# Keys and queries of both chunks transposed together, and one schedule for attention and both blocks

## The chip, the cores and the metric

The kernel runs on one core of a Trainium2 chip. The metric is the device time of one execution, in microseconds. Matrix products and transposes run on TensorE (PE in the profile; its weight loads are PEld), elementwise work on VectorE (DVE) and ScalarE (ACT), a few small copies on GpSimd (POOL), and SyncE (SP) issues all transfers.

## The reference

A linear attention with a complex decay per token and channel, followed by two blocks on the 3072 tokens x 384 channels that it gives: a gated one (SiLU) and one with the maximum of three products. All arithmetic is float32.

```python
def _attn_ref(q, k, v, a_re, a_im):        # 4 batches, 8 heads, 768 tokens, 48 channels
    mag = np.sqrt(a_re * a_re + a_im * a_im)
    scale = np.minimum(mag, 0.999) / (mag + 1e-06)
    a_re_n, a_im_n = (a_re * scale, a_im * scale)
    ...
    for t in range(S):
        new_re = ar * S_re - ai * S_im
        new_im = ar * S_im + ai * S_re
        kv = np.einsum('bhd,bhe->bhde', k[:, :, t], v[:, :, t])
        S_re, S_im = (new_re + kv, new_im)
        y[:, :, t] = np.einsum('bhd,bhde->bhe', q[:, :, t], S_re)
def _moe_ref(x, w_gate, w_val, w_out):     # 384 -> 1536 -> 384
    g = x @ w_gate
    return (g / (1 + np.exp(-g)) * (x @ w_val)) @ w_out
def _moe2_ref(x, w1, w2, w3, w_out):       # 384 -> 768 -> 384
    return np.maximum(np.maximum(x @ w1, x @ w2), x @ w3) @ w_out
```

## The kernel before

**The attention** is done in 12 units (`u`), three for each batch. A unit is 256 tokens of all 8 heads, two chunks of 128 tokens. Partition 64c + 8h + s of a unit's tiles holds chunk `c`, head `h` and block `s` of 16 consecutive tokens; the free axis holds the 16 tokens, real and imaginary part, and 48 channels. `decay` normalizes the decays and multiplies them up inside blocks; `prefix` transposes the blocks' totals on PE (`tq<-bt`), scans them on DVE, and `unfold` transposes the result back (`tq<-I`); `queries_keys` multiplies the scanned decays into queries (`Q`) and keys (in place, in `A`) and sends the keys to `kn` by 16 transfers. `attend` turns queries and keys so that the 96 rows of real and imaginary channels lie on partitions (`tp`, copied by ACT to `QT` and `KT`), and then for each chunk multiplies keys by queries (`sc`), masks on DVE (`P`), updates the state (`xs`) and forms the output (`ys`), which ACT copies to `xr`; heads 6 and 7 reach it through `y67` and six transfers.

In `turn` (line 920) one chunk is turned at a time: PE transposes 64 partitions x 96 columns, eight of them into one bank of PSUM, and ACT copies the bank with the tokens reordered. A unit takes four such groups for its queries and four for its keys, 768 transposes in the program. PSUM has 8 banks: `tq`, `tp`, `sc` and `ys` have one each, `acc` two, `g` and `v` one each.

**The first block** (`Moe1`) takes a unit's `xr` as soon as it is there: `make_x` splits it in a rounded part `xh` (ACT) and the rest `xl` (DVE), and `moe1_group` goes through six slices `f` of 256 hidden columns: `g` and `v` (18 matmuls each), SiLU on ACT, the product `sg` and the split `hh`, `hl`, and 18 matmuls into `acc`. Every product takes three matmuls, of rounded parts and rests. The weights come as 64-bit floats; DVE, ACT and in part PE convert and split them (`split_w`) in the first stage. **The second block** (`Moe2`) does the same for 512 tokens at a time: three products into `p`, maximum into `hs`, and 4 x 3 matmuls per hidden slice into four accumulators, which leave by `ot`.

**What sets the order.** `Plan` records every operation as a task (hence all of them have one line in the profile) and writes each engine's stream by a list schedule: of the tasks that are ready by estimated costs, the one with the longest remaining path goes first. On PE, an attention task that is ready goes first, and of the two blocks' tasks that are ready the one with the lowest turn number. Tiles with one tag share a ring of `bufs` buffers, in the order in which the program asks for them. Before, there are two such plans: the first ends with the attention of the last unit and the first block of units 0 to 9; then the attention's memory is given back, and the second plan holds the first block of units 10 and 11 and the whole second block.

Of the kernel before, what the change touches and what calls it, by code (L numbers as in the profile page):

```python
# [75 lines left out]
class Plan:  # L76
# [7 lines left out]
    PSUM_TAGS = ("g", "v", "acc", "tq", "tp", "sc", "ys", "p", "po0", "po1")  # L84
# [3 lines left out]
    def __init__(self, nc, direct=False):  # L88
        self.nc, self.direct = nc, direct
        self.tasks, self.tags, self.open = [], {}, None  # L90
        self.free = {e: 0.0 for e in self.LAT}
        self.free["sync"] = 0.65
        self.table = None
        self.moved = self.busy = 0.0
        self.tick, self.warm = -1, False
        self.raw = []

# [111 lines left out]
    def schedule(self):  # L209
# [19 lines left out]
        while True:  # L229
# [23 lines left out]
            t = self.tasks[i]  # L253
            if e in ("vector", "scalar", "gpsimd"):
# [167 lines left out]
class Moe1:  # L422
# [20 lines left out]
    def load(self, s):  # L443
        f0 = s * SL
        if self.packed is not None:
            DM = self.src["o"].shape[1]
            for n, a, c in (("g", self.KD, SL), ("v", self.KD, SL), ("o", 2, DM)):
# [67 lines left out]
class Moe2:  # L515
# [7 lines left out]
    def __init__(self, P, place, xplace, oplace, mp, pf, ws, wo, packed=None):  # L523
        self.packed = packed
        self.P, self.place, self.xplace, self.oplace, self.mp, self.pf = P, place, xplace, oplace, mp, pf
# [4 lines left out]

    def load(self, s):
        if self.packed is not None:
            for n, a, c in (("1", self.KD, SL), ("2", self.KD, SL), ("3", self.KD, SL), ("o", 2, self.DM)):
                self.wt[n, s] = load_packed(self.P, *self.place(n, s), a, c, self.packed[n][s])
            return
        for n in "123":
            x, m = cols(self.src[n], SL * s, SL)
            self.wt[n, s] = load_w(self.P, *self.place(n, s), self.KD, SL, (
                (0, 128, x.rearrange("(j p) f -> p j f", p=128)),), m)
        x, m = words(self.src["o"])  # L540
        self.wt["o", s] = load_w(self.P, *self.place("o", s), 2, self.DM, (
            (0, 128, x[SL * s:SL * s + SL].rearrange("(j p) e -> p j e", p=128)),), m)
# [16 lines left out]
    def hid(self, g, f, turn):  # L559
        P, mp, U = self.P, self.mp, self.U  # L560
        xh, xl = self.x[g]
        s, o = divmod(128 * f, SL)
        hs = P.tile(mp, [128, U], F32, "hs", 2)
        for n in "123":
            p = P.tile(self.pf, [128, U], F32, "p", 2)
# [10 lines left out]
        hh = P.tile(mp, [128, U], F32R, "h2h", 2)  # L576
        hl = P.tile(mp, [128, U], F32R, "h2l", 2)
        P.copy(hh, hs, U)
        P.split_lo("vector", hl, hs, hh, U)
        self.h[g, f] = hh, hl  # L580

    def out(self, g, f, turn, dst):
        P = self.P
        hh, hl = self.h.pop((g, f))
        w = self.wt["o", f // 2]
        for t in range(self.U // 128):
            if f == 0:
                pool, tag = self.oplace(t)
                self.acc[g, t] = P.tile(pool, [128, self.DM], F32, tag)
            ps, ts = self.acc[g, t], slice(128 * t, 128 * t + 128)  # L590
            P.task("tensor", turn)
            P.mm3(ps, (hh[:, ts], hl[:, ts]), (w[:, f % 2, 0], w[:, f % 2, 1]), f == 0, f == self.KF - 1, self.DM)
            P.close()
            if f == self.KF - 1:
                ot = P.tile(self.mp, [128, self.DM], F32, "ot", 2)
# [4 lines left out]
def general_path(tc, q, k, v, a_re, a_im, w_gate, w_val, w_out, w1, w2, w3, w2_out, out):  # L600
# [94 lines left out]
    with ExitStack() as s2:  # L695
# [4 lines left out]
        m2 = Moe2(P, lambda n, s: (wp, f"y{n}{s}"), lambda n, g: (mp, f"x2{n}"), lambda t: (po, f"po{t}"),  # L700
                  mp, pf, (w1, w2, w3), w2_out)
# [15 lines left out]
def attn_moe_kernel(ctx, tc, q, k, v, a_re, a_im, w_gate, w_val, w_out, w1, w2, w3, w2_out,  # L717
# [52 lines left out]
    def load_a(u):  # L770
        A = A_t[u] = T([128, L, 2, D], "A", 3)
# [52 lines left out]
    def prefix(u):  # L824
# [3 lines left out]
        pt = T([NP, 2, 128], "tq", 1, patt)  # L828
# [4 lines left out]
        t1, t2 = T([NP, 2, G, 8], "tt1"), T([NP, 2, G, 8], "tt2")  # L833
# [32 lines left out]
    def unfold(u):  # L866

        pt = T([128, 2, D], "tq", 1, patt)
# [291 lines left out]
```

## Time and profile before

| | |
|---|---|
| time, three runs | 1070.1, 1072.82, 1078.19 us |
| the profiled execution, its own time | 1078.24 us |
| its span, first to last instruction | 1076.5 us |
| mean granted TensorE clock | 0.974 |
| PE busy | 1008.0 us, 7607 matmuls |
| DVE busy | 712.7 us |
| ACT busy | 487.5 us |

The shares are means over stages that differ: in the first 92 us decays and weights are prepared, to 655 us attention and first block run side by side, to 765 us the first block of the last two units, and then the second block alone. A stage is read by its window, and a wait by the instruction that ended it.

### The profile page before, as it was taken

What the parts mean: (1) busy time and instruction counts of PE and PEld (TensorE: products, weight loads), DVE (VectorE), ACT (ScalarE), POOL (GpSimd) and SP (SyncE); (2) the same over time, 40 slices, a digit from 0 to 9 for tenths busy, and PEclk for the clock granted to TensorE, in tenths of its full rate; (3) what the DMA queues carried; (4) which work ended last, traced back from release to release, by engine and by line L of the source; (5) the groups of instructions that cost most, each with busy time, mean ns of one, the idle gap of its engine ahead of it and who ended that gap; (6) DMA issues with size and microseconds to landing.
All of it is one profiled execution on the core that took longest, in us unless ns stands there. A gap on an engine that the chain in (4) does not pass through costs nothing.

```text
span 1076.5 us, 18718 instructions
## 1 busy us (share of the span) xinstructions
PE 1008.0 (94%) x7607; PEld 925.2 (86%) x7607; DVE 712.7 (66%) x1551; ACT 487.5 (45%) x762; POOL 5.0 (0%) x31
## 2 busy tenths in 40 slices
PE   0596999979999999999999999999999999999996
PEld 0476998879999999999999999999988888888885
DVE  6989999897988787888778984488322232222221
ACT  4454755656656565666566555234212121221211
POOL 0000000000000000000000000000000000000000
PEclk9968999989999999999999999999999999999998
DMA  9630211303130303040303032344101010100000
GB/s 380 250 91 19 56 53 45 97 27 97 31 103 25 102 8 115 3 121 13 112 3 82 13 82 42 108 177 162 45 1 59 1 59 1 59 15 16 30 1 32
DMA packets 52799, 73.54 MB, mean 68 GB/s; under 512 B 29281, under 2 KB 45793, under 8 KB 52705
## 3 DMA queue, kind: packets, MB, share of 16 engines
q1 hardware_dynamic: 52704, 72.27, 21.2%
q8 instruction: 61, 1.00, 0.4%
q14 instruction: 34, 0.27, 0.1%
HBM read 52.20 MB, written 9.44 MB: 57 GB/s over the span
## 4 chain that ended last, share of the span: by engine, by line
PE 87%; DVE 7%; ACT 2%; DMA 2%; issue 1%; SPq 1%; ACTq 0%; DVEq 0%
PE p L176 21%; PE v L176 16%; PE g L176 16%; PE acc L176 15%; PE ys L176 6%; PE tp L176 5%; PE sc L176 4%; PE po L176 3%; DVE A L176 2%; DVE s L176 2%; DVE t L176 1%; DMA A<-in_a_u_dram 1%; ACT s L176 1%; SPq L176 1%; DVE xo L176 0%
## 5 line engine op out<-in xcount | busy, mean ns | idle before, releaser
L176 PE MATMUL g<-xh,wg 128*128 128x256 f32 x864 | 178.9, 291 | 8.4 <-ACT xh L176 7.4
L176 PE MATMUL acc<-hh,wo 128*128 128x256 f32 x864 | 176.2, 290 | 1.2 <-DVE wo L176 0.7
L176 PE MATMUL v<-xh,wv 128*128 128x256 f32 x864 | 175.1, 289 | 2.2 <-DVE sg L176 2.2
L176 DVE TENSOR_TENSOR hs<-hs,p 128x512 f32<-128x512 f32 x72 | 49.5, 688 | 190.2 <-PE p L176 190.2
L176 PEld LDWEIGHTS g<-xh,wg 128*128 128x128 f32 x864 | 144.2, 195 | 11.8 <-ACT xh L176 7.9
L176 PEld LDWEIGHTS v<-xh,wv 128*128 128x128 f32 x864 | 142.4, 194 | 5.2 <-DVE sg L176 2.4
L176 PEld LDWEIGHTS acc<-hh,wo 128*128 128x128 f32 x864 | 142.0, 193 | 4.9 <-DVE wo L176 1.1
L176 PE MATMUL g<-xl,wg 128*128 128x256 f32 x432 | 124.2, 287 | 4.5 <-DVE xl L176 4.5
L176 PE MATMUL acc<-hl,wo 128*128 128x256 f32 x432 | 123.0, 285 | 0.1
L176 PE MATMUL v<-xl,wv 128*128 128x256 f32 x432 | 123.1, 285 | 0.0
L176 PE MATMUL p<-wv,y 128*128 128x512 f32 x324 | 112.4, 395 | 0.0
L176 ACT CAST hh<-sg 128x512 fp32r<-128x512 f32 x72 | 44.6, 620 | 109.4 <-PE acc L176 101.3
L176 DVE TENSOR_TENSOR sg<-sg,v 128x512 f32<-128x512 f32 x72 | 49.4, 686 | 60.4 <-PE v L176 46.9
L176 PEld LDWEIGHTS g<-xl,wg 128*128 128x128 f32 x432 | 84.2, 195 | 5.4 <-DVE xl L176 5.3
L176 ACT CAST h2h<-hs 128x512 fp32r<-128x512 f32 x36 | 22.4, 621 | 140.2 <-DVE hs L176 140.2
L176 PEld LDWEIGHTS acc<-hl,wo 128*128 128x128 f32 x432 | 83.5, 193 | 0.4 <-DVE hl L176 0.3
L176 PEld LDWEIGHTS v<-xl,wv 128*128 128x128 f32 x432 | 83.8, 194 | 0.0
L176 PEld LDWEIGHTS p<-wv,y 128*128 128x128 f32 x324 | 60.8, 188 | 13.7
L176 ACT ACT_TABLE_LOAD x53 | 68.0, 1283 | 5.7 <-DVE hl L176 2.6
L176 PE MATMUL p<-wg,y 128*128 128x512 f32 x216 | 69.7, 394 | 0.0
L176 ACT COPY KT<-tp 96x512 f32<-96x512 f32 x48 | 50.3, 1048 | 38.4 <-PE tp L176 21.3
L176 ACT ACTIVATE sg<-g 128x512 f32<-128x512 f32 x72 | 43.1, 598 | 44.7 <-PE g L176 38.2
(195 smaller groups left out, 1928.3 us busy)
## 6 DMA issues: line engine op xcount, KB each, us to landing
A<-in_a_u_dram SPq DMA_DIRECT2D x12, 768.0 KB
qk<-in_qk_u_dram SPq DMA_DIRECT2D x12, 768.0 KB
kn<-A SPq DMA_DIRECT2D x192, 48.0 KB
vt<-in_v_u_dram SPq DMA_DIRECT2D x24, 204.0 KB
wg<-in_moe_w_gate_s_dram SPq DMA_DIRECT2D x6, 768.0 KB
wv<-in_moe_w_val_s_dram SPq DMA_DIRECT2D x6, 768.0 KB
wo<-in_moe_w_out_s_dram SPq DMA_DIRECT2D x6, 768.0 KB
x2d<-xo SPq DMA_DIRECT2D x12, 384.0 KB
```

What stands on the lines that cost most here:

```text
L176: getattr(getattr(self.nc, eng), name)(**k)
```

## The change

- `turn` takes both chunks together: 128 partitions x 96 columns a transpose, four of them in one bank; eight are one task and fill two banks (`tp` has two, and `tq` is gone: the transposes of `prefix` and `unfold` take `tp` too). 384 transposes take the place of 768. ACT makes four copies of 512 columns for the queries of a unit and four for the keys, from a bank read across its four transposes to runs of four words.
- The whole program is one list schedule. The second block's weights and tiles take buffers of the attention (`A0`, `A1`, `qk`, `QT`, `KT`, `P`, `t3`, ...) and of the first block's weights, and `p` and two accumulators take banks of the attention.
- `A` has two buffers for units in turn (before three), `xr` two (before one), `ot` four (before two); the scan's `tt1`, `tt2` come from the ring `s3` of the decays. The weights' conversion rotates four buffers, two of them in the place of the last `wo`, which is therefore loaded later.
- The order in which a unit's parts are asked for is `U0 Q0 A0 D1 P1` throughout, and the planner counts 0.27 us for a change of kind on PE.

```diff
-    PSUM_TAGS = ("g", "v", "acc", "tq", "tp", "sc", "ys", "p", "po0", "po1")
+    PSUM_TAGS = ("g", "v", "acc", "tq", "tp", "sc", "ys", "p", "acc0", "acc1", "acc2", "acc3")
...
+            if e == "tensor":
+                now += 0.27 if t[4] is None and not self.odd else 0.0
+                self.odd = t[4] is None
...
     def load_a(u):
-        A = A_t[u] = T([128, L, 2, D], "A", 3)
+        A = A_t[u] = T([128, L, 2, D], f"A{u % 2}")
...
-        pt = T([NP, 2, 128], "tq", 1, patt)
+        pt = T([NP, 2, 128], "tp", 2, patt)
...
-        t1, t2 = T([NP, 2, G, 8], "tt1"), T([NP, 2, G, 8], "tt2")
+        t1, t2 = [s3()[0:NP].rearrange("p l d -> p (l d)")[:, 0:16 * G].rearrange("p (c g s) -> p c g s", c=2, s=8) for _ in range(2)]
...
-        def turn(src, nm, bufs, c):
-            t = T([NP, H, C], nm, bufs)
+        def turn(src, nm):
+            t = T([NP, 128, L], nm)
             for i in range(2):
-                pt = T([NP, 8, 64], "tp", 1, patt)
+                pt = [T([NP, 4, 128], "tp", 2, patt) for _ in range(2)]
                 P.task("tensor")
                 for l in range(8):
-                    P.transpose(pt[:, l], src[64 * c:64 * c + 64, 8 * i + l].rearrange("p c d -> p (c d)"),
-                                ident[64 * c:64 * c + 64, 64 * c:64 * c + 64], 0.062)
+                    P.transpose(pt[l // 4][:, l % 4], src[:, 8 * i + l].rearrange("p c d -> p (c d)"), ident, 0.099)
                 P.close()
-                P.copy(t.rearrange("p h (s l) -> p l (h s)", l=L)[:, 8 * i:8 * i + 8], pt, 1200)
-            return t
+                for j in range(2):
+                    ls = slice(8 * i + 4 * j, 8 * i + 4 * j + 4)
+                    P.copy(t[:, :, ls], pt[j].rearrange("p l n -> p n l"), 635)
+            return lambda c, h: t[:, 64 * c + 8 * h:64 * c + 8 * h + 8].rearrange("p s l -> p (s l)")
-        QT = [turn(Q_t[u], "QT", 2, c) for c in range(2)]
-        xr = xr_t[u] = T([128, 3, U], "xr", 1, mp)
+        qt, kt = turn(Q_t[u], "QT"), turn(A_t[u], "KT")
+        xr = xr_t[u] = T([128, 3, U], "xr", 2, mp)
...
-            o = "U0 Q0 D1 P1 A0" if u < 2 else "D1 U0 P1 Q0 A0"
+            o = "U0 Q0 A0 D1 P1"
...
-            if u < NU - 2:
-                moe1_group(u)
-            elif u < NU - 1:
-                moe1.make_x(u, xr_t[u])
-        P.flush()
-        at.close()
+            moe1_group(u)
...
+        homes = {"1": ("A0", "wv0", "wo1"), "2": ("A1", "wo0", "wg2"), "3": ("wg0", "wg1", "wv2"), "o": ("qk", "wv1", "wo2")}
+        roles = {"xh": slab("wg3", "wo3"), "xl": slab("wv3", "wg4"), "x": att(sb, 1, "Q"), "hs": att(sb, 2, "P"),
+                 "h": att(sb, 1, "QT", "KT"), "ot": att(sb, 4, "t3"), "p": att(patt, 2, "tp"), "dec": att(sb, 1, "kn0", "kn1"),
+                 "acc": lambda i: ((patt, "ys", 1), (pacc, "acc", 1), (pgv, "g", 1), (pgv, "v", 1))[i]}
```

How the order moves is shown at three places. On PE, a unit's turn in the middle of the attention; before, two of its groups, with the neighbours that stand around each (`tp<-ident,Q` are transposes of queries, `g`, `v`, `acc` the first block's matmuls):

```order
L176 MATMUL g<-xh,wg_1160 128x256
L176 MATMUL tp<-ident,Q 96x64 x8
L176 MATMUL g<-xh,wg_1160 128x256
...
L176 MATMUL v<-xh,wv_1348 128x256
L176 MATMUL tp<-ident,Q 96x64 x8
L176 MATMUL acc<-hh,wo_1418 128x256
```

And in the changed kernel, a unit's second group of queries and its two groups of keys (`tp<-ident,A_3297`):

```order
L177 MATMUL g<-xh,wg_652 128x256
L177 MATMUL tp<-ident,Q 96x128 x8
L177 MATMUL g<-xh,wg_652 128x256
...
L177 MATMUL v<-xh,wv_632 128x256
L177 MATMUL tp<-ident,A_3297 96x128 x8
L177 MATMUL acc<-hh,wo_534 128x256
...
L177 MATMUL acc<-hh,wo_534 128x256
L177 MATMUL tp<-ident,A_3297 96x128 x8
L177 MATMUL g<-xh,wg_1053 128x256
```

The groups still stand alone between the first block's matmuls, but there are four in a unit where there were eight, of 128 columns each.

On DVE, from the third unit's last mask product (`P`) to the rest of its input (`xl`), before (`s_1978`, `s_2012` and `A<-A` are a later unit's decays, `t_...<-BP,G` and `t_...<-A,G` the fourth unit's `unfold` and `queries_keys`):

```order
L176 TENSOR_TENSOR P<-sc,mask 128x512
L176 TENSOR_SCALAR s_1978<-s_2012 128x768
L176 SCALAR_TENSOR_TENSOR okacc<-M,okacc 96x16
L176 SCALAR_TENSOR_TENSOR s_1978<-s_2012,s_1978 128x768
L176 TENSOR_TENSOR A<-A,s_1978 128x768
L176 TENSOR_TENSOR t_2254<-BP,G 128x288
L176 TENSOR_TENSOR t_2256<-BP,G 128x288
L176 TENSOR_TENSOR t_2259<-A,G 128x384
L176 TENSOR_TENSOR t_2262<-A,G 128x384
...
L176 TENSOR_TENSOR xl<-xr,xh 128x768
```

And now (`I`, `s_2013`, `s_2025`, `Vn`, `tv` are the fourth unit's scan):

```order
L177 TENSOR_TENSOR P<-sc,mask 128x512
L177 TENSOR_TENSOR s_1969<-BP 128x192
L177 TENSOR_TENSOR BP<-s_1969 128x2x48 x2
L177 TENSOR_TENSOR s_2013<-I 96x32x7
...
L177 TENSOR_TENSOR hl<-sg,hh 128x512
...
L177 TENSOR_TENSOR ph<-I,ea 96x32
L177 TENSOR_TENSOR sg<-sg,v 128x512
L177 TENSOR_TENSOR tv<-ph,Vn 96x16 x2
L177 TENSOR_TENSOR Vn<-tv 96x8 x2
L177 TENSOR_TENSOR xl<-xr,xh 128x768
```

The fourth unit's scan, which stood ahead of the last mask product, now stands behind it, and the fourth unit's queries behind `xl`.

On PE at the same place, the end of the third unit's attention (`ys`) and its first `g`, before:

```order
L176 MATMUL ys<-QT,xs_103 64x128 x2
L176 MATMUL tq<-ident,I 128x48 x2
L176 MATMUL acc<-hh,wo_1527 128x256
...
L176 MATMUL acc<-hh,wo_1527 128x256
L176 MATMUL g<-xh,wg_219 128x256
L176 MATMUL g<-xl,wg_219 128x256
```

And now, `wg_971` being the second unit's last slice and `wg_229` the third unit's first:

```order
L177 MATMUL ys<-QT,xs_103 64x128 x2
L177 MATMUL tp<-ident,bt 96x128 x2
L177 MATMUL acc<-hh,wo_705 128x256
...
L177 MATMUL g<-xh,wg_971 128x256
...
L177 MATMUL v<-xh,wv_1240 128x256
...
L177 MATMUL acc<-hh,wo_735 128x256
L177 MATMUL g<-xh,wg_229 128x256
```

Between the attention's end and that `g` stood 18 matmuls of `acc`; now there stand 63 of the second unit's (9 and 18 of `acc`, 18 of `g`, 18 of `v`).

## Rows read from the trace of the kernel before

**Rows 1.** The page, busy time: engine, us, share of the span, instructions.
```profile
PE 1008.0 (94%) x7607; PEld 925.2 (86%) x7607; DVE 712.7 (66%) x1551; ACT 487.5 (45%) x762; POOL 5.0 (0%) x31
```

**Rows 2.** Windows: length, busy us of PE, PEld, DVE, ACT, POOL; clock, DMA share, GB/s.
```profile
92.00:219.40 127.40, 118.55 (x1026) 111.44 (x1026) 118.03 (x267) 70.98 (x114) 1.20 (x4) 0.95 0.20 55
219.40:226.50 7.10, 0.70 (x3) 0.29 (x1) 7.10 (x18) 1.63 (x2) 0.00 (x0) 0.65 0.21 67
226.50:231.60 5.10, 5.05 (x23) 5.05 (x24) 5.10 (x13) 2.50 (x4) 0.00 (x0) 0.50 0.00 0
231.80:655.00 423.20, 423.20 (x3923) 402.89 (x3922) 354.84 (x871) 266.88 (x415) 2.10 (x9) 1.00 0.21 59
655.00:765.00 110.00, 109.73 (x952) 107.81 (x951) 67.83 (x94) 39.72 (x57) 0.00 (x0) 1.00 0.37 124
```

**Rows 3.** Groups on PE: shapes, count, busy us, mean ns, idle before.
```profile
L176 PE MATMUL tp<-ident,A 64*96 64x64 f32 x384 | 32.5, 227 | 1.5 <-ACT KT L176 1.5
```

**Rows 4.** Timeline of PE, two transposes among `g` and `v`: start, length.
```profile
299.85 0.28 PE L176 MATMUL g<-xh,wg 128*128 128x256 f32 x1
300.06 0.65 PE L176 MATMUL tp<-ident,A 64*96 64x64 f32 x8
300.64 0.39 PE L176 MATMUL g<-xh,wg 128*128 128x256 f32 x1
300.87 0.28 PE L176 MATMUL g<-xl,wg 128*128 128x256 f32 x1
...
301.70 0.28 PE L176 MATMUL g<-xh,wg 128*128 128x256 f32 x1
301.82 0.38 PE L176 MATMUL tq<-ident,bt 128*96 128x128 f32 x2
302.16 0.28 PE L176 MATMUL v<-xl,wv 128*128 128x256 f32 x1
```

**Rows 5.** Timeline of PE, from `g` into `sc` and `ys`.
```profile
466.49 0.28 PE L176 MATMUL g<-xh,wg 128*128 128x256 f32 x1
466.61 1.05 PE L176 MATMUL sc<-QT,KT 96*128 96x128 f32 x8
467.50 1.50 PE L176 MATMUL ys<-vt,kn 128*96 128x72 f32 x16
```

**Rows 6.** Timeline of DVE, ACT and PE, the third unit's way into the first block.
```profile
215.05 0.69 DVE L176 TENSOR_TENSOR P<-sc,mask 128x512 f32<-128x512 f32 x1 [0.29 <-PE sc L176]
222.89 0.83 ACT L176 CAST xh<-xr 128x768 fp32r<-128x768 f32 x1 [2.53 <-DMA xr<-y]
225.54 0.96 DVE L176 TENSOR_TENSOR xl<-xr,xh 128x768 fp32r<-128x768 f32 x1
226.55 0.58 PE L176 MATMUL g<-xl,wg 128*128 128x256 f32 x1 [2.20 <-DVE xl L176]
```

**Rows 7.** Groups on DVE: a small one of the scan, one of the first block.
```profile
L176 DVE TENSOR_TENSOR tv<-ph,Vn 96x16 f32<-96x16 f32 x48 | 6.1, 166 | 0.8
L176 DVE TENSOR_TENSOR hl<-sg,hh 128x512 fp32r<-128x512 f32 x72 | 49.7, 690 | 19.1 <-ACT hh L176 17.9
```

**Rows 8.** Groups on ACT: the reordering copy, and a plain one of 512 columns.
```profile
L176 ACT COPY KT<-tp 96x512 f32<-96x512 f32 x48 | 50.3, 1048 | 38.4 <-PE tp L176 21.3 <-PE sc L176 17.1
L176 ACT COPY hs<-p 128x512 f32<-128x512 f32 x36 | 21.1, 587 | 84.3 <-PE p L176 84.3
```

**Rows 9.** Timeline of ACT, the last copies out of the accumulators.
```profile
1064.47 1.01 ACT L176 COPY ot<-po 128x384 f32<-128x384 f32 x2 [1.30 <-PE po L176]
1068.69 0.48 ACT L176 COPY ot<-g 128x384 f32<-128x384 f32 x1 [3.20 <-DMA out_dram<-ot]
```

**Rows 10.** Timeline of PE, transposes into the scan (first unit) and back (two units).
```profile
24.08 0.64 PE L176 MATMUL tq<-ident,bt 128*96 128x128 f32 x2 [24.08 <-ACT bt L176]
...
34.24 0.43 PE L176 MATMUL tq<-ident,I 48*128 48x48 f32 x2 [4.85 <-DVE I L176]
317.07 0.32 PE L176 MATMUL tq<-ident,I 48*128 48x48 f32 x2
```

More of the change, by code (lines that the diff above doesn't have):

```diff
@@ L96, in __init__ @@
         self.raw = []
+        self.odd = True
     def tile(self, pool, shape, dtype, tag, bufs=1):
@@ L441, in rows, with load @@
         return (0, D, h6[0]), (64, D, h6[1]), (48, 16, h67[0]), (112, 16, h67[1])
-    def load(self, s):
+    def load(self, s, which="gvo"):
         f0 = s * SL
@@ L446, in load @@
             DM = self.src["o"].shape[1]
-            for n, a, c in (("g", self.KD, SL), ("v", self.KD, SL), ("o", 2, DM)):
+            for n in which:
+                a, c = (2, DM) if n == "o" else (self.KD, SL)
                 self.wt[n, s] = load_packed(self.P, self.wp, f"w{n}{s}", a, c, self.packed[n][s])
@@ L521, with __init__ @@
     U = 512
[L523 to L525 removed]
+    def __init__(self, P, place, ws, wo, packed=None):
+        self.P, self.place, self.packed = P, place, packed
+        self.count = {}
         self.src = dict(zip("123", ws), o=wo)
@@ L529, in __init__, with tile @@
         self.wt, self.x, self.h, self.acc = {}, {}, {}, {}
+    def tile(self, role, shape, dtype=F32, i=None):
+        if i is None:
+            i = self.count[role] = self.count.get(role, -1) + 1
+        pool, tag, bufs = self.place(role, i)
+        return self.P.tile(pool, shape, dtype, tag, bufs)
     def load(self, s):
@@ L575, in hid @@
                 P.tt("vector", hs, hs, p, ALU.max, U)
[L576 to L580, printed above, removed]
+        h = self.h[g, f] = self.tile("h", [128, 2, U], F32R)
+        P.copy(h[:, 0], hs, U)
+        P.split_lo("vector", h[:, 1], hs, h[:, 0], U)
     def out(self, g, f, turn, dst):
         P = self.P
-        hh, hl = self.h.pop((g, f))
+        h = self.h.pop((g, f))
         w = self.wt["o", f // 2]
@@ L587, in out @@
             if f == 0:
-                pool, tag = self.oplace(t)
-                self.acc[g, t] = P.tile(pool, [128, self.DM], F32, tag)
+                self.acc[g, t] = self.tile("acc", [128, self.DM], i=t)
             ps, ts = self.acc[g, t], slice(128 * t, 128 * t + 128)
             P.task("tensor", turn)
-            P.mm3(ps, (hh[:, ts], hl[:, ts]), (w[:, f % 2, 0], w[:, f % 2, 1]), f == 0, f == self.KF - 1, self.DM)
+            P.mm3(ps, (h[:, 0, ts], h[:, 1, ts]), (w[:, f % 2, 0], w[:, f % 2, 1]), f == 0, f == self.KF - 1, self.DM)
             P.close()
             if f == self.KF - 1:
-                ot = P.tile(self.mp, [128, self.DM], F32, "ot", 2)
+                ot = self.tile("ot", [128, self.DM])
                 P.copy(ot, ps, self.DM)
@@ L699, in general_path, with place @@
         po = s2.enter_context(tc.tile_pool(name="gpo", bufs=1, space=PSUM))
-        m2 = Moe2(P, lambda n, s: (wp, f"y{n}{s}"), lambda n, g: (mp, f"x2{n}"), lambda t: (po, f"po{t}"),
-                  mp, pf, (w1, w2, w3), w2_out)
+        def place(role, i):
+            if role in "123o" or role == "acc":
+                return po if role == "acc" else wp, f"{role}{i}", 1
+            return pf if role == "p" else mp, role, 1 if role[0] == "x" else 2
+        m2 = Moe2(P, place, (w1, w2, w3), w2_out)
         for s in range(m2.NS):
@@ L988, in moe1_group @@
     def moe1_group(u):
-        if u not in moe1.x:
-            moe1.make_x(u, xr_t[u])
+        moe1.make_x(u, xr_t[u])
         for f in range(moe1.NS):
@@ L1014, in attn_moe_kernel @@
         for s in range(moe1.NS):
-            moe1.load(s)
+            moe1.load(s, "gvo" if s < moe1.NS - 1 else "gv")
             if s == 2:
@@ L1023, in attn_moe_kernel @@
         prefix(0)
-        whole = T([128, 2, 768], "A", 3)
-        dec = [T([128, 768], "xo", 1, mp), Part(whole, 0), Part(whole, 1)]
+        last = moe1.NS - 1
+        whole = P.tile(wp, [128, 2, 768], F32, f"wo{last}")
+        dec = [T([128, 768], "xo", 1, mp), T([128, 768], "xr", 2, mp), Part(whole, 0), Part(whole, 1)]
+        nd = 0
         for s in range(moe1.NS):
-            for i, n in enumerate("gvo"):
+            if s == last:
+                for x in dec[2:]:
+                    x.whole_done()
+                moe1.load(s, "o")
+            for n in "gvo":
                 pe = s < 3
@@ L1030, in attn_moe_kernel @@
                     bank = T([128, 3, U], "acc", 1, pacc)
-                moe1.split(n, s, dec[i], (bank, ident, nident) if pe else "vector")
-        for x in dec[1:]:
-            x.whole_done()
+                moe1.split(n, s, dec[nd % (4 if s < last else 2)], (bank, ident, nident) if pe else "vector")
+                nd += 1
         for u in range(NU):
-            o = "U0 Q0 D1 P1 A0" if u < 2 else "D1 U0 P1 Q0 A0"
+            o = "U0 Q0 A0 D1 P1"
             for w in o.split():
@@ L1086, in attn_moe_kernel @@
         P.flush()
-        n2.close()
+        at.close()
         p1.close()
```

50 lines of the change are left out of this document (22 added, 28 removed).

## The prediction

> **What bounds the kernel now.** I read the busy times first: TensorE works for 94% of the span, VectorE 66%, ScalarE 45% [rows 1]. A mean over stages says nothing of a stage, so the windows come next [rows 2]. From 231.8 us on TensorE never stands still until the end of the second block: 423.2 us busy of 423.2, then 109.73 of 110, while VectorE has room (354.84 of 423.2). In that part the time is the sum of what TensorE is given, and only less work there shortens it. From 92 to 219.4 us TensorE and VectorE are both nearly full (118.55 and 118.03 of 127.4). [...] The third unit's last mask product starts at 215.05, its output reaches `xh` at 222.89, `xl` only starts at 225.54, 1.8 us after `xh` is through (222.89 + 0.83), because other VectorE work stands ahead of it, and the first full `g` runs at 226.55.
>
> **Part 1: the transposes.** In the timeline a group of eight 64-row transposes stands between block matmuls [rows 4]. From 300.87 to 301.70 seven of these take 0.12 us each. From 299.85 to 300.87 two of them and the group take 1.02, so the group costs 0.78. It streams for (0.65 - 0.23) / 7 = 0.06 us a transpose, the 0.23 being the length of one alone [rows 3], 0.48 for eight. The other 0.30 is spent on going in and out. The two 128-row transposes of the same rows cost 302.16 - 301.70 - 0.24 = 0.22, which is 0.11 each and nothing for going in or out. The same holds for `sc` [rows 5]: 0.12 after the `g` before it, and (467.50 - 466.61) / 8 = 0.11 for each of its eight passes. So the 0.30 belongs to operands of 64 rows or 64 columns (`tp` before, the transposes back from the scan, the `ys` of 64 columns), not to leaving the first block's matmuls.
>
> Counted in the order of the instructions, such small operands form 118 separate runs before and 45 after. That is 73 x 0.30 = 21.9 us. Streaming goes from 768 x 0.06 + 24 x 0.11 = 48.7 to 408 x 0.11 = 44.9. TensorE is given 25.7 us less. It matters where: 87 of the runs before and 32 after lie behind the third unit's first `g`, where TensorE is full. There it is 55 x 0.30 = 16.5, streaming 576 x 0.06 + 16 x 0.11 = 36.3 against 304 x 0.11 = 33.4, and a group of 18 `acc` matmuls that now comes behind that `g` costs 2.2: 16.5 + 2.9 - 2.2 = **17.2 us less**. Ahead of it TensorE has 25.7 - 17.2 = 8.5 less.
>
> [...]
>
> **Part 2: the third unit's entry.** VectorE's order ahead of the third unit's last mask product loses 29 instructions of the fourth unit's scan, 7 of decays and 3 of the first block, 39 in all. At 0.16 us for the scan's small ones and 0.69 for a block's [rows 7], 0.47 for a decay's and less 0.08 where one overlaps the next, that is 9.8 us; at the stretch's mean of 118.03 / 267 = 0.44 it would be 17. I take 9.8, as the instructions are known. The product then comes at 215.05 - 9.8 = 205.25. From there to the full `g` it was 226.55 - 215.05 = 11.5, less the 1.8 for which `xl` stood behind the fourth unit's queries, which now come later: 9.7, hence 214.95. TensorE itself is ready at 219.4 - 8.5 = 210.9, if it idles as much before that as it did. The later one decides: 226.55 - 214.95 = **11.6 us** gained, with ends 0 (VectorE is late for another reason) and 15.6 (TensorE's own 210.9). The slow clock of 5.1 us did 23 matmuls, worth 2.6 at 0.11 to 0.12; half of the 2.5 lost is taken, **1.3**, as a wait of 4 us stays, with ends 0 and 2.5.
>
> **Part 3: the end.** The third copy to `ot` waited 3.20 us for the landing of the first one's transfer [rows 9]. With four buffers it follows the second, at 1064.47 + 1.01 = 1065.5 instead of 1068.7. Of these 3.2 I take **3.0 us**, as the last accumulator's matmuls end a little after that.
>
> **What I put at nothing.** ScalarE's copies: 96 of 1.05 us become 96 of between 0.59 (plain) and 1.05 [rows 8]. Words go out in runs of four, so a quarter of the jumps and of the surplus: 0.70. TensorE waits for two of them before the next group; 18 to 27 block matmuls lie between, 2.2 to 3.2 us, which cover 1.4. At 1.05 the copies take 2.1 plus the hand-over: up to 0.9 us a unit, 10 in all, an end of the range. The load of `A` now waits for the keys two units back and stands on SyncE's queue behind 16 transfers of keys, almost a unit ahead of its use. The second block's weights come into buffers that fall free late; from the last `ys` to the first `p` there are 23 groups of 18 matmuls, 50 us, and the first three conversions stand near their beginning. GpSimd's few copies don't move past anything.
>
> **Sum.** 17.2 + 11.6 + 1.3 + 3.0 = 33.1. The profiled execution took 1078.2 us, 1.7 more than its span, and gives 1045.1; it is the slow end of the three runs, whose median, 1072.8, gives 1039.7. I forecast **1042**.
>
> **The rivals.** (a) *The entry does not come sooner* (0.11): the third unit is held by something else at 226.5, as both engines were full before it. Only parts 1 and 3 are left: 1042 + 12.9 = 1055. (b) *The scan becomes the wait* (0.07). The transposes into and back from it now share the two banks of `tp`, and 90 block matmuls lie between, 10.8 us; one unit took 317.07 - 301.82 = 15.2 before [rows 4, 10], though nothing pressed it. The fastest took 34.24 - 24.08 = 10.2 with other work in between. At 13 us a unit, 2.2 x 11 = 24: 1066. (c) *The 0.30 belongs to any change away from the block's matmuls* (0.03): such changes only go from 118 to 100, and three quarters of 55 x 0.30 is lost, 1054; `sc` without such a cost speaks against it [rows 5]. (d) *Slower: the copies hold TensorE* (0.04). Two banks, both filled by each group, leave no spare one. With 10.8 us of cover for the four groups of a unit, the gain is gone where 8 copies take 10.8 + 31 / 12 = 13.4, from 1.7 us a copy. At 2.1, twice the old price, since a copy now jumps on both sides, it is (16.8 - 10.8) x 12 = 72: 1114. Nothing in the trace reads a bank across, so it can't be excluded. [...] (e) *The hand-over stalls, or the change does less than it says* (0.05): if the three weights of the first `p` are late, TensorE waits for their 12 instructions of 67.83 / 94 = 0.72 us [rows 2], 8.7 in all: 1051.
>
> **How the numbers follow.** 0.70 is left for the forecast, 1030 to 1052: below by the ends of part 2 (4.0 and 1.2), the median's base and a little more idle time recovered ahead of 210.9, above by the copies' 10. The range, **1030 to 1060**, takes in (a), (c) and (e) and leaves out (b) and (d) and a little of the rest. 1% of 1072.8 is 11, about what a measurement here can tell: faster means below 1062. It holds nearly all of the forecast, (a), (c) and (e) and a third of (b): 0.87; within 1%: 0.09; slower: 0.04.
>
> **What would show it.** Right: TensorE's transposes of 96 x 128 at 0.11 us with 0.12 before and after; the third unit's first full `g` near 215 us; hardly any idle time on TensorE from there on; the last four `ot` copies in a row; some 17 us less between that `g` and the last matmul. Wrong: idle time in front of `tp`, with `QT` or `KT` copies as the releaser (d), in front of the `tp` back from the scan (b), or in front of the first `p` (e); copies above 1.05 us.

## The result, and the profile after

The changed kernel takes 1040.21 us (median of four runs, 1039.16 to 1041.22) against 1072.17 for the one before (four runs, 1070.1 to 1078.19): 0.9681 of its time, 95% interval 0.9651 to 0.9712. Forecast were 1042 us, in a range of 1030 to 1060.

Busy time on the page of the changed kernel; the columns are those of [rows 1]:

```profile
PE 973.3 (94%) x7223; PEld 908.5 (87%) x7223; DVE 712.7 (69%) x1551; ACT 432.9 (42%) x750; POOL 12.3 (1%) x31
```

VectorE does what it did, to the tenth; TensorE does 34.7 us less and ScalarE 54.6. TensorE's share is still 94%, so the kernel has become shorter with the same bound. The windows, to be laid beside [rows 2]:

```profile
92.00:206.00 114.00, 106.58 (x898) 101.97 (x897) 105.64 (x240) 58.86 (x104) 0.91 (x3) 0.93 0.22 62
206.00:215.00 9.00, 9.00 (x74) 8.63 (x73) 6.63 (x30) 4.25 (x8) 1.64 (x1) 1.00 0.03 7
215.00:231.80 16.80, 16.80 (x143) 16.80 (x142) 15.35 (x33) 13.07 (x22) 0.00 (x0) 1.00 0.07 24
231.80:655.00 423.20, 421.90 (x3795) 412.83 (x3794) 359.45 (x881) 221.52 (x395) 8.03 (x9) 1.00 0.23 63
655.00:765.00 110.00, 109.73 (x828) 103.64 (x826) 72.81 (x100) 40.13 (x63) 0.00 (x0) 1.00 0.35 117
```

The 7.1 us in which TensorE stood still after 219.4, and the 5.1 at a granted clock of 0.50, are gone: from 206 to 231.8 it is busy all the time at 1.00. Behind that it is nearly as full as before (421.90 of 423.20 us to 655). The third unit's way into the first block (VectorE, ScalarE, TensorE), as in [rows 6]:

```profile
200.49 0.68 DVE L177 TENSOR_TENSOR P<-sc,mask 128x512 f32<-128x512 f32 x1
208.97 0.83 ACT L177 CAST xh<-xr 128x768 fp32r<-128x768 f32 x1 [0.77 <-PE v L177]
210.17 0.96 DVE L177 TENSOR_TENSOR xl<-xr,xh 128x768 fp32r<-128x768 f32 x1
210.93 0.28 PE L177 MATMUL g<-xh,wg 128*128 128x256 f32 x1
211.19 0.39 PE L177 MATMUL g<-xl,wg 128*128 128x256 f32 x1
```

The first `g` takes its place behind other matmuls with no wait shown, and the rest `xl` is through just as its turn comes. One group of keys on TensorE, beside [rows 4]:

```profile
290.30 0.29 PE L177 MATMUL v<-xh,wv 128*128 128x256 f32 x1
290.42 1.03 PE L177 MATMUL tp<-ident,A 128*96 128x128 f32 x8
...
291.42 0.28 PE L177 MATMUL acc<-hl,wo 128*128 128x256 f32 x1
```

Read as before the change, from the matmul ahead to the second one behind, less two of 0.12: 291.42 - 290.30 - 0.24 = 0.88 for both chunks, where one chunk cost 0.78. It is eight times 0.11, with nothing for going in or out.

### The profile page after: what moved, and what is told of

Same layout as the page of the kernel before. It is cut to its first block, busy times and chain, and to the rows that moved or that the text cites. A ratio compares the mean times of both kernels' runs of the same rounds, so it can differ in the third digit from the quotient of the medians.

```text
span 1039.5 us, 17981 instructions
## 1 busy us (share of the span) xinstructions
PE 973.3 (94%) x7223; PEld 908.5 (87%) x7223; DVE 712.7 (69%) x1551; ACT 432.9 (42%) x750; POOL 12.3 (1%) x31
## 4 chain that ended last, share of the span: by engine, by line
PE 81%; DVE 12%; ACT 2%; SPq 2%; DMA 1%; issue 1%; ACTq 0%; DVEq 0%
PE tp L177 25%; PE g L177 15%; PE v L177 15%; PE acc L177 15%; PE ys L177 8%; PE sc L177 4%; DVE s L177 3%; DVE A L177 2%; DVE t L177 2%; SPq L177 2%; DVE wo L177 1%; DVE xr L177 1%; DVE xo L177 1%; DMA xr<-y 1%; DVE xl L177 1%
## 5 line engine op out<-in xcount | busy, mean ns | idle before, releaser
L177 PE MATMUL g<-xh,wg 128*128 128x256 f32 x864 | 173.0, 287 | 4.3 <-ACT xh L177 4.1
L177 DVE TENSOR_TENSOR P<-P,tp 128x512 f32<-128x512 f32 x72 | 49.5, 688 | 178.7 <-PE tp L177 178.7
L177 PEld LDWEIGHTS g<-xh,wg 128*128 128x128 f32 x864 | 141.5, 193 | 5.2 <-ACT xh L177 4.5
L177 PE MATMUL tp<-wg,wg 128*128 128x512 f32 x162 | 57.4, 391 | 0.0
L177 ACT COPY P<-tp 128x512 f32<-128x512 f32 x36 | 21.1, 587 | 81.6 <-PE tp L177 81.6
L177 PE MATMUL sc<-QT,KT 96*128 96x128 f32 x384 | 53.3, 282 | 1.7 <-DVE P L177 1.7
L177 DVE TENSOR_TENSOR hl<-sg,hh 128x512 fp32r<-128x512 f32 x72 | 49.5, 687 | 4.7 <-ACT hh L177 4.7
L177 PEld LDWEIGHTS sc<-QT,KT 96*128 96x128 f32 x384 | 46.9, 192 | 4.5 <-DVE P L177 2.2
```

Of the source, the lines that this page charges most:

```text
L177: getattr(getattr(self.nc, eng), name)(**k)
```

## The experiments

Each was timed against the kernel before on the same chip; differences from 1040.21 are between medians. The runs were made in three rounds, in which the kernel before had medians of 1072.75 (experiments 2 to 5), 1076.47 (1 and 6 to 8) and 1073.66 (9 to 12), beside the 1072.17 above, so a difference of 2 or 3 us between rounds is not shown by the medians alone.

**1. The kernel before once more.** No edit. 

> The kernel before, unchanged, profiled once more: its shown execution took 1078.2 us, about 6 more than its median. [...]

This one execution took 1074.18 us. Rows of its PE, DVE and ACT timelines:

```profile
88.79 0.58 PE L176 MATMUL g<-xh,wg 128*128 128x256 f32 x1 [3.16 <-ACT xh L176]
211.28 0.69 DVE L176 TENSOR_TENSOR P<-sc,mask 128x512 f32<-128x512 f32 x1 [0.28 <-PE sc L176]
222.77 0.58 PE L176 MATMUL g<-xl,wg 128*128 128x256 f32 x1 [2.20 <-DVE xl L176]
1060.80 1.00 ACT L176 COPY ot<-po 128x384 f32<-128x384 f32 x2 [1.31 <-PE po L176]
```

From the full `g` to the first `ot` copy it took 838.03 us, in the execution shown earlier 837.92 [rows 6, 9]. So that one lost its 3.8 us ahead of the third unit's full `g` and nothing behind it. I had put the loss at the third unit's entry, with its full `g` at 220 to 222 here. But it lost them at another place, for its very first `g` is late already:

```profile
92.12 0.58 PE L176 MATMUL g<-xh,wg 128*128 128x256 f32 x1 [3.17 <-ACT xh L176]
```

Of the 3.8 us, 92.12 - 88.79 = 3.3 were lost in the first stage, where decays and weights are prepared. The third unit's wait for `xl` is 2.20 in both, and both run some 5.1 us at a granted clock of 0.50 behind it.

**2. grouped64: the transposes by halves again, the order of instructions kept.**

```diff
-                    P.transpose(pt[l // 4][:, l % 4], src[:, 8 * i + l]..., ident, 0.099)
+                for c in range(2):
+                    for l in range(8):
+                        P.transpose(pt[c][:, l], src[cs, 8 * i + l]..., ident[cs, cs], 0.0495)
```

> The changed kernel with its order of instructions kept, but each 128-row transpose given back as two of 64 rows: in each group eight of the first chunk, then eight of the second, one chunk to a bank; the copies read a bank of one chunk. Theory (the price lies in going into and out of operands of 64 rows): small-operand runs go from 45 to 92, 47 x 0.30 = 14.1 us, streaming from 41.7 to 43.2 us, 15.6 in all; 12 of the 48 groups lie ahead of the third unit's input, where a part is hidden. 1040.2 + 12 to 16: 1052 to 1056, and TensorE's first full g of the third unit later by 0 to 4 us. If going from the first chunk's rows to the second's costs a second 0.30: 1064 to 1070. Rival (the gain came from the single schedule and the order, not from the transposes): 1040 to 1043.

1045.78 us, 0.9753 of before (0.9737 to 0.9770): 5.6 more than the changed kernel, less than half of the 12 to 16 that the theory asked for. TensorE's rows say why:

```profile
291.81 0.28 PE L177 MATMUL v<-xh,wv 128*128 128x256 f32 x1
292.02 0.92 PE L177 MATMUL tp<-ident,A 64*96 64x64 f32 x16
...
293.09 0.28 PE L177 MATMUL acc<-hl,wo 128*128 128x256 f32 x1
```

The sixteen cost 293.09 - 291.81 - 0.24 = 1.04, and the first eight alone would cost 0.78. The second eight take other rows of TensorE and run partly beside the first. The starts of the sixteen in such a group, in ns from the first one's, show it:

```
first chunk:  0  96  152  208  264  320  375  431
second chunk:             270  366  422  478  534  590  645  701
```

(The two chains are told apart by the signal that the eighth of each gives to ScalarE, at 431 and 701.) The second chunk begins 6 ns behind the first one's fifth. So 1.04 - 0.88 = 0.16 a group was left to lose, 7.7 for 48 groups and 5.8 for the 36 from the fourth unit's on, in place of the 15.6 expected. My theory held what was true of the kernel before, where a group has one chunk's rows, for a law.

**3. paired64: as 2, but the two chunks' transposes alternate.**

```diff
+                for l in range(8):
+                    for c in range(2):
+                        P.transpose(pt[c][:, l], src[cs, 8 * i + l]..., ident[cs, cs], 0.0495)
```

> As grouped64, but the transposes of the two chunks alternate, so that neighbours take different rows of TensorE. Theory A (64-row transposes stand one behind another whatever rows they take, as the eight of a group before): the same time as grouped64, 1052 to 1056. Theory B (two that take different rows run side by side): streaming is halved, 21.6 us instead of 43.2, against the 15.6 of grouped64: 1040 - 6 = 1034, from 1031 to 1040. [...] Theory C (each change of rows has a price like that of going in): at 0.15 to 0.30 for each of 720 changes, above 1140.

1036.05 us (1035.79 to 1036.2), 0.9661 (0.9645 to 0.9677): theory B.

```profile
292.36 0.28 PE L177 MATMUL acc<-hh,wo 128*128 128x256 f32 x1
292.57 0.65 PE L177 MATMUL tp<-ident,A 64*96 64x64 f32 x16
...
293.37 0.28 PE L177 MATMUL g<-xl,wg 128*128 128x256 f32 x1
```

Sixteen cost 293.37 - 292.36 - 0.24 = 0.77, what eight cost before: the two halves run side by side and the way in and out is paid once. 48 x (0.88 - 0.77) = 5.3 would be the gain on the changed kernel, 4.2 was measured. Its runs lie below all of the changed kernel's, though the intervals of the two ratios overlap a little; the traces bear the gain out, with 815.49 us from the third unit's full `g` to the last matmul against 820.05. The copies cost the same (0.58), so they are not the reason. It is the fastest version tried.

**4. mixed: single 64-row transposes between 128-row ones, order kept.**

```diff
+                for l, c in ((0, 2), (1, 0), (2, 2), (1, 1), (3, 2), (5, 0), (4, 2), (5, 1), (6, 2), (7, 2)):
+                    cs = slice(64 * c, 64 * c + 64) if c < 2 else slice(0, 128)
```

> The changed kernel, order kept; in each group of eight 128-row transposes two are given as two of 64 rows each, and these four stand singly between 128-row ones. Two token positions of each eight land in exchanged places, so the output differs. Theory (every run of small operands costs 0.30, whatever stands around it): runs go from 45 to 237, 192 x 0.30 = 57.6 us, streaming unchanged; 48 of the runs lie ahead of the third unit's input, where a part is hidden: 1040.2 + 43 to 58, 1083 to 1098. Rival c of the prediction (the price belongs to any change away from the block's matmuls): a group has one such change as in the changed kernel, 1040 to 1044. Rival (the price is paid once for a group that holds any small operand): 48 x 0.30 = 14, 1052 to 1056.

1087.52 us, 1.0127 (1.0099 to 1.0155): 47.3 more, inside the theory's 43 to 58 and far from both rivals.

```profile
298.14 0.28 PE L177 MATMUL v<-xh,wv 128*128 128x256 f32 x1
298.26 2.11 PE L177 MATMUL tp<-ident,Q 128*96 128x128 f32 x10
...
300.33 0.28 PE L177 MATMUL acc<-hl,wo 128*128 128x256 f32 x1
```

A group costs 300.33 - 298.14 - 0.24 = 1.95, which is 1.07 more than eight 128-row ones for four runs that stream as much: 0.27 a run, among transposes alone. The price belongs to the change of operand height, not to leaving the block's matmuls.

**5. copy1: the copies to QT and KT write single words.**

```diff
-                    P.transpose(pt[l // 4][:, l % 4], src[:, 8 * i + l]..., ident, 0.099)
+                    P.transpose(pt[l // 4][:, l % 4], src[:, 2 * i + l // 4 + 4 * (l % 4)]..., ident, 0.099)
-                    ls = slice(8 * i + 4 * j, 8 * i + 4 * j + 4)
+                    ls = slice(2 * i + j, L, 4)
```

> The changed kernel, order kept; a bank takes every fourth token position (0, 4, 8, 12 and so on) instead of four neighbours, so that ScalarE's copies to QT and KT write single words 16 bytes apart instead of runs of four. Nothing else differs. The copies take 0.58 us in the changed kernel. Theory (the old price of 1.05 came from words that go out singly, and the matmuls between two groups cover it): 0.9 to 1.05 us a copy, time 1040 to 1043, hardly any idle time of TensorE with QT or KT as the releaser. Rival d of the prediction (copies of that length hold TensorE): 0.9 us a unit or more, 1049 to 1055. Rival (the copy is bound by its 512 columns and not by the pattern): 0.58 us, 1040. [...]

1048.54 us, 0.9775 (0.9758 to 0.9792): 8.3 more. Groups on ACT, the changed kernel's copies first:

```profile
L177 ACT COPY QT<-tp 96x512 f32<-96x512 f32 x48 | 26.3, 574 | 9.2 <-PE tp L177 9.2
L177 ACT COPY KT<-tp 96x512 f32<-96x512 f32 x48 | 25.6, 581 | 4.2 <-PE tp L177 4.2
```

and those of copy1:

```profile
L177 ACT COPY QT<-tp 96x512 f32<-96x512 f32 x48 | 50.8, 1116 | 4.8 <-PE tp L177 4.8
L177 ACT COPY KT<-tp 96x512 f32<-96x512 f32 x48 | 49.1, 1134 | 0.3 <-PE tp L177 0.3
```

Same reads, same columns; only the writes differ, and a copy takes 1.13 in place of 0.58. TensorE then waits for the keys (timeline of copy1):

```profile
298.03 0.28 PE L177 MATMUL g<-xh,wg 128*128 128x256 f32 x1
298.50 1.16 PE L177 MATMUL sc<-QT,KT 96*128 96x128 f32 x8 [0.19 <-ACT KT L177]
299.49 1.50 PE L177 MATMUL ys<-vt,kn 128*96 128x72 f32 x16
...
302.13 0.28 PE L177 MATMUL v<-xl,wv 128*128 128x256 f32 x1
```

The same place in the changed kernel:

```profile
296.36 0.28 PE L177 MATMUL g<-xh,wg 128*128 128x256 f32 x1
...
299.77 0.28 PE L177 MATMUL v<-xl,wv 128*128 128x256 f32 x1
```

From the `g` to the second `v`, less two of 0.12, it is 3.86, where the changed kernel takes 3.17 (299.77 - 296.36 - 0.24). So a copy of this length is not covered here. My theory of cover fell. The rival's price of 0.9 us a unit was about right: from the third unit's full `g` to the last matmul the run takes 827.95 us in place of 820.05, 7.9 for nine units, and the time lies 0.5 us below the rival's range. The shorter copy is a part of the gain.

**6. split64: part 1 undone in full, in the single schedule.**

```diff
-                pt = [T([NP, 4, 128], "tp", 2, patt) for _ in range(2)]
+                pt = T([NP, 8, 64], "tp", 2, patt)
-        qt, kt = turn(Q_t[u], "QT"), turn(A_t[u], "KT")
+        QT = [turn(Q_t[u], f"QT{c}", 1, c) for c in range(2)]
+            KT = turn(A_t[u], "KT", 1, c)
```

> The changed kernel with the transposes of the kernel before in full: one chunk at a time, eight of 64 rows to a task, one bank, with its copies to runs of single words; single schedule, order of parts and all buffers as in the changed kernel (the list schedule places the 96 tasks anew). Theory (part 1 is a sum over TensorE's work: 59 more runs of 0.30 and 1.7 of streaming, 19.4 us in all, 15 to 16 of it behind the third unit's input): 1055 to 1061. By the group prices of the traces, 1.54 for two groups of one chunk against 0.877, 48 x 0.66 = 32 would be the upper end, 1072, if none of the 96 stood beside other small operands. Rival (schedule and order carry the gain): 1040 to 1046, like grouped64.

1057.04 us, 0.9830 (0.9788 to 0.9873): 16.8 more, within the theory's 1055 to 1061. The third unit's first `g` starts at 212.0 and its full one at 212.56, only 1.1 and 1.4 later than in the changed kernel. From there to the last matmul it is 833.5 us in place of 820.0, 13.5 more, where 15 to 16 were expected. The copies take 1.08 again, as in the kernel before, but TensorE stands still no longer than in the changed kernel (1.3 us against 1.6), while in copy1 it was 5.0: the 13.5 us are work of the transposes, and not waits for the copies, as far as the trace shows.

**7. order: the old order of a unit's parts in the changed kernel.**

```diff
-            o = "U0 Q0 A0 D1 P1"
+            o = "U0 Q0 D1 P1 A0" if u < 2 else "D1 U0 P1 Q0 A0"
```

> The changed kernel with the old order in which a unit's parts are asked for (U0 Q0 D1 P1 A0 for two units, then D1 U0 P1 Q0 A0); all else as changed. On VectorE the third unit's rest xl then stands 26 instructions later than in the changed kernel, about where it stood before. [...] Rival (the entry came earlier because TensorE had less to do ahead of it, 8.5 us): first g at 211 to 214, 1040 to 1043.

1079.81 us, 1.0043 (1.0020 to 1.0066): 39.6 more, as slow as the kernel before or a little slower, and far beyond both expectations. Mine had the third unit's first `g` at 218 to 224 and a time of 1048 to 1054, as 26 instructions of VectorE at the mean of 0.44 us [rows 2] are 11 us. TensorE in the first stage of this kernel:

```profile
68.52 0.63 PE L177 MATMUL tp<-ident,bt 128*96 128x128 f32 x2
...
70.01 1.91 PE L177 MATMUL tp<-ident,Q 128*96 128x128 f32 x8
```

The first unit's queries, at 49.49 in the changed kernel, stand at 70.01, behind the transposes `bt` of the second unit's scan. The two share the ring `tp` now, which serves in the order of asking, and the old order asks for the second unit's scan first. The first `g` comes at 110.8 in place of 89.2, the third unit's at 228.3; from there to the last matmul it is 18.4 us longer, with TensorE busy for 395.55 of 408 us from 232 to 640.

**8. join_q: the queries' transposes joined in the kernel before.**

```diff
-        QT = [turn(Q_t[u], "QT", 2, c) for c in range(2)]
+        qt = turn2(Q_t[u], "QT")
```

(`turn2` is the changed kernel's `turn`; `tq` becomes `tp` with two buffers.) 

> The kernel before with the joined, 128-row transposes for the queries alone (tp two banks, tq in tp); keys, both plans, order and buffers as before. Theory: small-operand runs go from 118 to 78, 40 x 0.30 = 12 us, streaming 0.7; some 9 to 10 of it behind the third unit's input, which VectorE's order (xl 8 instructions later) puts 0 to 4 us later: 1072.4 - 9.5 + 0 to 4 = 1062 to 1067. Rival (joining pays only with the single schedule): 1070 to 1075.

1066.07 us, 0.9906 (0.9873 to 0.9939), as the theory had it. From the third unit's full `g` to the last matmul it is 827.1 us (226.38 to 1053.5) instead of 839.2 (222.77 to 1062.0 in experiment 1). Of these 12 us some 2.3 are the stretch at the granted clock of 0.50, which this kernel does not have behind its full `g` (1.00 from 226.38 on); 9.8 are left for the 31 runs fewer that lie there, where the theory had 9 to 10. The full `g` itself is 3.6 later, within the theory's 0 to 4, but for another reason: the queries stood behind `bt` as in 7 (66.57 and 68.34), and the very first `g` came at 105.7 in place of 88.8.

**9. best: paired64 with still fewer runs.**

```diff
-            P.transpose(pt[:, i], F_t[u][0:D, i]..., ident[0:D, 0:D], 0.08)
+            P.transpose(pt[:, i], F_t[u][:, i]..., ident[0:NP, 0:NP], 0.08)
-                if pr % 2 == 0:
+                if pr == 0:
                     P.task("tensor")
```

> paired64 (64-row transposes of both chunks side by side) with fewer runs of small operands: the transposes back from the scan take all 96 rows (the lower 48 repeat the upper ones) instead of 48, and a chunk's eight ys heads are one task instead of two. Runs go from 92 to 70. Theory (0.30 a run, wherever): 22 x 0.30 = 6.6 less, 24 x 0.04 = 1 more of streaming: 1036 - 5.5 = 1030.5, from 1029 to 1033. Rival (the wider task delays what waits for it, or the two kinds of run have no such price): 1036 to 1040.

1043.44 us, 0.9713 (0.9667 to 0.9759): 7.4 more than paired64. The wider transposes out of the scan cost 0.20 a pair as a group in place of 0.44, as expected. But the third unit's full `g` comes 3.1 later than in paired64 (214.29 against 211.15), and from it to the last matmul it is 820.3 us in place of 815.5. The task of sixteen `ys` waits for all of a chunk's masked products, and the schedule moved:

```profile
PE sc L177 <- DVE P L177: 4.9, 4, 3.5
PE g L177 <- DVE wg L177: 2.4, 1, 2.4
```

These are waits of TensorE from 92 us on (total, times, longest) that paired64 does not have; one of 3.5 us stands behind 640 us. Which of the two edits brought each was not separated.

**10. ot2: two buffers for the last copies.**

```diff
-                 ... "ot": att(sb, 4, "t3"), ...
+                 ... "ot": att(sb, 2, "P"), ...
```

> The changed kernel with the last copies going out through two buffers (those of P) instead of four of t3; nothing else. Theory: the third copy waits for the landing of the first one's transfer as before, 2.9 to 3.2 us: 1043 (1042 to 1044), no difference ahead of the last matmul. Rival (the last transfer's own landing sets the end whichever buffer it leaves from): 1040 to 1041.

1066.45 us, 0.9929 (0.9905 to 0.9953): the edit did more than it should, since `hs` lives in `P` too and waited for the transfers of every token group's copies. TensorE's waits from 700 us on, and the last copies:

```profile
PE tp L177 <- ACT P L177: 15.4, 5, 4.1
```

```profile
1055.19 0.48 ACT L177 COPY P<-ys 128x384 f32<-128x384 f32 x1 [1.36 <-PE ys L177]
...
1059.07 0.48 ACT L177 COPY P<-g 128x384 f32<-128x384 f32 x1 [2.93 <-DMA out_dram<-P]
```

The total says nothing of part 3, but the end can be read: the third copy waits 2.93 us, and from the first copy to the end of the span it is 1066.8 - 1055.19 = 11.6 us; the changed kernel takes 1039.5 - 1030.02 = 9.5.

**11. twoplans: the schedule cut in two as before.**

```diff
+            if u == NU - 2:
+                P.flush()
             moe1_group(u)
```

> The changed kernel with the list schedule cut as before, ahead of the first block of the tenth unit (counted from 0); buffers, order of parts and transposes as changed. Theory (TensorE is full on both sides of that place, so one schedule or two makes no difference): first full g of the third unit at 210.9 as in the changed kernel, 1040 to 1043. Rival (the single schedule itself fills TensorE there): 1046 or more, with idle time of TensorE after 620 us.

1042.9 us, 0.9710 (0.9666 to 0.9754): the theory, at its upper end. The third unit's first `g` is at 211.0. The 2.7 us more are hardly clear, as they lie between two rounds and the intervals of the two ratios overlap. In the profiled executions the last matmul starts at 1034.7 in place of 1031.2. TensorE stands still for 1.3 us more from 640 to 765 (it is busy for 123.47 of 125 us, in the changed kernel for 124.73), with waits of 0.46 and 0.34 ahead of `acc` at 640.47 and 641.19. Where the rest goes was not found.

**12. neworder: the new order of parts in the kernel before.**

```diff
-            o = "U0 Q0 D1 P1 A0" if u < 2 else "D1 U0 P1 Q0 A0"
+            o = "U0 Q0 A0 D1 P1"
```

> The kernel before with the new order of a unit's parts (U0 Q0 A0 D1 P1) alone. On VectorE the third unit's xl moves 11 instructions forward (28 in the changed kernel), and TensorE gets 12 more small-operand runs, 3.6 us. Theory (the entry follows VectorE's order): full g of the third unit 11 x 0.44 = 5 us earlier, 217 to 219 against 222.8, the stretch behind it up to 3 longer: 1070 to 1075, no clear gain without the joined transposes. Rival (the order is what the change gains by, as its loss in the changed kernel was 39 us): 1062 or less.

1084.42 us, 1.0081 (1.0050 to 1.0111): 10.8 more than the median of before in the same runs (5 to 12 by the interval), where little change was expected. The third unit's entry:

```profile
224.23 0.58 PE L176 MATMUL g<-xh,wg 128*128 128x256 f32 x1 [5.17 <-ACT xh L176]
225.22 0.58 PE L176 MATMUL g<-xl,wg 128*128 128x256 f32 x1 [0.41 <-DVE xl L176]
```

The wait for `xl` fell from 2.20 to 0.41, but `xh` itself comes no sooner, and the stretch behind is 12 us longer. So neither order of parts helps the other kernel's buffers.

## Why the prediction was right

The three terms, from the rows of the changed kernel, those of the execution that the prediction used [rows 6, 9], and those of experiment 1:

| | forecast | against the execution used | against experiment 1 |
|---|---|---|---|
| third unit's full `g` earlier | 11.6 | 226.55 - 211.19 = 15.4 | 222.77 - 211.19 = 11.6 |
| from it to the first `ot` copy | 17.2 + 1.3 | 837.92 - 818.83 = 19.1 | 838.03 - 818.83 = 19.2 |
| the end | 3.0 | 12.0 - 9.5 = 2.5 | 11.7 - 9.5 = 2.2 |
| sum | 33.1 | 37.0 | 33.0 |
| difference of their times | | 1078.24 - 1041.12 = 37.1 | 1074.18 - 1041.12 = 33.1 |

(818.83 is 1030.02, the first of the last four copies below, less 211.19.)

Of the signs that the prediction named, the transposes at 0.11 us, the four copies in a row and the full TensorE came. The full `g` came at 211.19 and not near 215. For what follows, windows of the stretch from the first unit's `g` to the third unit's full `g`: experiment 1 (and the 5 us behind that stretch), the changed kernel, split64 and mixed, in this order, with the columns of [rows 2]:

```profile
88.79:222.77 133.98, 118.91 (x1027) 111.44 (x1028) 125.26 (x283) 72.32 (x115) 1.20 (x4) 0.93 0.20 56
222.77:227.90 5.13, 5.13 (x24) 5.13 (x25) 5.13 (x13) 2.58 (x4) 0.00 (x0) 0.50 0.00 0
89.20:211.19 121.99, 113.30 (x944) 108.22 (x944) 113.02 (x265) 60.61 (x108) 0.91 (x3) 0.93 0.21 58
89.89:212.56 122.67, 114.29 (x1009) 108.70 (x1007) 111.08 (x246) 67.32 (x108) 3.09 (x3) 0.93 0.21 58
89.63:223.45 133.82, 126.73 (x959) 114.11 (x959) 113.52 (x265) 60.97 (x108) 3.49 (x3) 0.89 0.19 53
```

**The slow clock** (0.50 for 5.1 us, [rows 2]) was mis-sized. The prediction gave back half of it, 1.3, as TensorE was to wait 4 us for the third unit still. No such wait is left, and the granted clock is 1.00 there: the 24 matmuls that took 5.13 us take 2.9 at 0.12, so 2.3 came back.

**Part 1** was right in size and in kind: without the clock's 2.3 it is 19.2 - 2.3 = 16.9, where 17.2 was forecast. The 128-row groups cost 0.88 with no way in or out, a run of small operands costs 0.24 to 0.29 (0.77 - 8 x 0.06 = 0.29 in experiment 3, 0.27 in 4, 0.44 - 0.20 = 0.24 in 9), and undoing it all brings 16.8 us back. The joined groups depend on short copies: copy1 shows that with copies of 1.13 about 8 us would have gone to waits. The prediction priced the copies at 0.70 and the cover as enough for that; they take 0.58. Runs of four words take about the plain price of 0.59 [rows 8], single words 1.13 (copy1).

**Joining is not the best that was tried.** A 128-row group beats two 64-row groups of one chunk each, 0.88 against 2 x 0.78. But where neighbours take different rows, two do run side by side (paired64, 0.77 for both chunks, with the two halves given in turn), and for the same order of instructions that is 4.2 us faster than what the change does.

**Part 2** was 3.8 us too small against the execution that it was worked out from, near the end of 15.6 that the prediction gave it. Against experiment 1 it is right to the tenth, and that is luck, for two errors of 1.0 cancel. The last mask product came 211.28 - 200.49 = 10.8 sooner (9.8 forecast), but from it to the full `g` it is 211.19 - 200.49 = 10.7, where 9.7 was forecast: `xl` no longer stands 1.8 us behind other work but 0.4 (210.17 - 208.97 - 0.83), while `xh` comes 8.5 us behind the product and not 7.8. Nor did VectorE alone decide: TensorE reached the `g` in its turn at 210.93.

What brought this is shown only in part. In the windows above, TensorE was busy for 118.9 us of the 134.0 in experiment 1 and stood still for 15.1; in the changed kernel it is 113.3 of 122.0, and 8.7. So the 12.0 us are 5.6 of busy time and 6.4 of standing still. VectorE's order is not enough by itself: mixed has the changed kernel's order, and with TensorE busy for 126.7 us (some of it at a lower clock, 0.89 in the mean) its full `g` comes at 223.45. The opposite test is weak, for split64 gives the 64-row transposes back and keeps 212.56, but there TensorE is only 1.0 us busier in this stretch, and not the 8.5 that the prediction counted ahead of the `g`. Nor was it the single schedule (twoplans, full `g` at 211.24). The order of parts alone does not do it in the buffers of before, and without the order the changed kernel loses 39.6. It takes both, and which of the buffers matter (two of `xr`, two of `A`, the scan's tiles in `s3`, the conversion's four) stays open.

**Part 3** was mis-sized by 0.5 to 0.8. The last four copies stand in a row as forecast:

```profile
1030.02 0.48 ACT L177 COPY t<-ys 128x384 f32<-128x384 f32 x1 [1.31 <-PE ys L177]
1030.55 0.48 ACT L177 COPY t<-acc 128x384 f32<-128x384 f32 x1
1031.08 0.48 ACT L177 COPY t<-g 128x384 f32<-128x384 f32 x1
1031.61 0.48 ACT L177 COPY t<-v 128x384 f32<-128x384 f32 x1
```

The third stands 1.06 behind the first, before 4.22 [rows 9], so the copies win 3.2. But from the last one's start to the end of the span it is 7.9 us now and was 7.4, which I had not counted. The issue of the four transfers on SyncE shows why (start, length of all four), now and, with the last copy, in experiment 1:

```profile
1030.53 3.46 SPq L177 DMA_DIRECT2D out_dram<-t  x4
1065.07 0.48 ACT L176 COPY ot<-v 128x384 f32<-128x384 f32 x1
1061.31 5.61 SPq L176 DMA_DIRECT2D out_dram<-ot  x4
```

The issues end at 1033.99 and 1066.92. From the last copy's start to there it is 2.4 now and was 1.8; from there to the end of the span it is 5.5 and was 5.6. So what the four transfers lose by standing close together is lost in their issue, not in the landing of the last.

**At nothing** was right for the hand-over: TensorE is busy for 109.73 of 110 us from 655 to 765, as before. Whether the single schedule is worth something there (2.7 us by twoplans, which lie within the 19.2) is not clear of the noise. **The rivals**: the entry came (a), the scan held nothing (b), mixed rules out (c), and (d) did not come because the copies are short, while its mechanism is there at 0.9 us a unit.

## What to carry to other kernels

On TensorE count the runs of operands of half height, not only the instructions: each cost 0.24 to 0.30 us here, 0.27 where it was a single transpose (mixed), and inside a run the two halves are best given in turn, as they then work side by side (0.77 us a group in paired64, 1.04 one half behind the other in grouped64). A copy that takes four neighbouring words from four transposes cost 0.58 us here, one that scatters single words 1.13 (copy1), and with the joined groups the slow copy held TensorE for 0.9 us a unit. Where operations share a ring of buffers, the order in which the program asks for them is a schedule of its own: change the order and the sharing together, and take the base of a sum from more than one execution.

## What the runs showed of the hardware

- Sixteen 64-row transposes with the two halves of the rows in turn took 0.65 us in paired64, as long as eight of one half before [rows 4]. With one half behind the other, in grouped64, sixteen took 0.92: the second half's first started 6 ns behind the first half's fifth, and ahead of its sixth (the starts in experiment 2).
- In the changed kernel ScalarE read a bank of PSUM across its four transposes (one word every 512 bytes) at the price of a plain copy, 0.58 us for 512 columns against 0.59 [rows 8]; single words written 16 bytes apart cost 1.12 to 1.13 (copy1), those 64 bytes apart before, read without jumps, 1.05 to 1.06 [rows 8].
- A transpose pair with 96 rows (best) cost 0.20 us between matmuls, where one with 48 rows (paired64) cost 0.44: more rows, less than half the time.
